# Block 0 of a fused attention and leaky-ReLU feed-forward kernel: one-level Strassen products in three of its four chunks, cut into slots, with the sums of w_out made there

## The chip, the cores and the metric

The kernel runs on one core of a Trainium2 chip. The metric is device time in microseconds for one execution, lower is better. The engines of the core are called here as the profile calls them: PE (TensorE, matmuls; PEld its weight loads), DVE (VectorE), ACT (ScalarE), POOL (GpSimd) and SP (SyncE, which here only issues transfers).

## The reference

A linear attention without softmax is followed by a feed-forward block with a leaky ReLU. The inputs q, k, v are float32; w_in and w_out are float64.

```python
# q, k, v: (8, 8, 576, 64) float32
kv  = einsum('bhsd,bhse->bhde', k, v)
out = einsum('bhsd,bhde->bhse', q, kv)
out = out / sqrt(mean(out * out, axis=-1) + 1e-6) * g_norm
x = out.transpose(0, 2, 1, 3).reshape(4608, 512)
h = x @ w_in                 # w_in (512, 2048) float64
g = maximum(0.01 * h, h)
y = g @ w_out                # w_out (2048, 512) float64, y (4608, 512)
```

## The kernel before

**Blocks and chunks.** The 4608 rows of x are worked in nine blocks of 512 rows (`NB = 9`). Within a block the 2048 hidden columns are four chunks (`NC = 4`); a chunk c has two halves h and two units u of 128 columns, so it needs four pieces of w_in (`w1_sb[h][c][:, u]`) and four of w_out (`w2_rows(h, c, u)`), 128x512 each.

**Weights.** The weights are read as 64-bit words and rounded to float32 on the chip. There are 32 jobs in the list `w_jobs`, one for each piece. For a job, `load_w` issues the transfer of 512 KB on SP into one of seven staging places, and `round_w` makes ACT convert the low word (L271, "add") and the high word (L269, "cut"), and then DVE clamp the high part (L273), shift it (L278), put its sign in (L280) and add the low part (L285). The first five jobs are rounded in `first_attention`; `first_block` calls `between` twice for every unit, and `between` loads and rounds the rest, two to three ahead of the unit that needs them. The jobs alternate between w_in and w_out.

**Block 0** (`first_block`) is the plain product. For each of 16 units n it computes one h tile of 128x512 (four matmuls of 512 columns), has ACT apply the leaky ReLU (L1353), and adds the product with w_out into four accumulators (`accs`), one unit late. Attention steps for block 1 and the tail of attention for block 0 are put in between by a dictionary of places.

**Block 1** uses one level of Strassen's method (Winograd's form, seven products): `product_h` computes a chunk of h, `product_o` a chunk of the output. Each of the seven products is 8 matmuls of 256 columns. A block is 28 slots, 7 for each chunk; in a slot one h product and, two slots behind (`LAG = 2`), one o product are issued. The sums that the products need are made by DVE and POOL: of x by `sides_x`, of w_in by `sides_w1` (four POOL additions of 128x512 a chunk), of w_out by `sides_w2` (four POOL additions a chunk, then written to DRAM for later blocks), of g by `sums_of` (four POOL additions a chunk). `combine` makes second-level sums of w_in for blocks 2 to 8, which use two levels for h.

**Order.** The instructions of each engine run in the order in which they are issued. `pin` keeps an instruction in the order of the program on its engine; all matmuls go through it (L121), and so do all steps of the rounding. `add` (L709) issues every sum, on DVE or POOL, and pins it if asked to or if `steady` is set. `put_off(n, f)` calls f after n slots.

Between block 0 and block 1 the kernel makes the sums of block 1's x on DVE, holds part of the w_in sums on POOL until the last weight is rounded (two copies of one element at L1405), and makes the w_out sums of chunk 0 on POOL; those of chunks 1 to 3 are made in block 1, each while `product_o` of the chunk before it runs.

Of the kernel before, what the change touches and what calls it, by code (L numbers as in the profile page):

```python
# [11 lines left out]
U32 = mybir.dt.uint32  # L12
I64 = mybir.dt.int64
# [11 lines left out]
def kernel(  # L25
# [41 lines left out]
    E = 32  # L67
# [26 lines left out]
    steady = first_done = in_line = False  # L94

    def in_turn(ins):

        if steady or in_line:
            pin(ins)

# [126 lines left out]
    def spare(n, name, dtype=F32):  # L227
# [3 lines left out]
    raw_homes = itertools.cycle([view(stage, i * NW, NW) for i in range(3)]  # L231
                                + [pair(i, NW) for i in range(4)])
# [15 lines left out]
    def load_f64(src, eng):  # L248
        raw = next(raw_homes).bitcast(U32)
        load(split(raw, src), src, eng)  # L250
        return raw.rearrange("p (n two) -> p n two", two=2)
# [44 lines left out]
    w_jobs[1:-1] = [w_jobs[i + 1 if i % 2 else i - 1] for i in range(1, len(w_jobs) - 1)]  # L296
# [3 lines left out]
    def load_w(j, *eng):  # L300
        eng = eng or (nc.sync,)
        dst, src = w_jobs[j]
        if w_in.dtype == I64:
            w_raws[j] = load_f64(src.bitcast(U32), eng)
        else:
            load(split(dst.rearrange("p a n -> p (a n)"), src) if len(src.shape) == 4 else dst,
                 src, eng)
# [5 lines left out]
    def round_w(j):  # L313
        for _ in rounding(j):
            pass

# [73 lines left out]
    def outputs(b, lo, hi, e, sums, kv=None):  # L390


        x, n = x_of(lo, hi), hi - lo
        tiles = att_tiles("o_ps")
        o_ps = [t[:, :n] for t in tiles]
        o_products(b, lo, hi, e, o_ps)
        if kv is not None:
            kv_beside(b + 1, kv, tiles)
        for l in range(2):
            sq = t2k(n, "sq" if e else f"sum{l}")  # L400
            nc.scalar.activation(sq, o_ps[l], func=AF.Square)
            if e == 0:
                sums.append(sq)
            else:
                in_turn(nc.vector.tensor_add(sums[l], sums[l], sq))
        for l in range(2):
            nc.scalar.activation(x[:, 2 * l + e, :], o_ps[l], func=AF.Copy, scale=g_sb[:, e:e + 1])

    def divide(lo, hi, sums):
# [3 lines left out]
        for l in range(2):  # L413
            t = t2k(n, "turned")
            in_turn(nc.vector.transpose(t, sums[l]))
            in_turn(nc.vector.tensor_reduce(rms[:, l, :], t.rearrange("p (a i) -> p a i", i=E),
                                            axis=AX.X, op=ALU.add))
            if l:
                act = nc.scalar.activation(rms, rms, func=AF.Sqrt, scale=1.0 / D, bias=eps_sb)
                if first_done:  # L420
                    pin(act)
            yield
        in_turn(nc.vector.reciprocal(rms, rms))
        spread = []
        for l in range(2):
            t = t2k(n, "spread")
            nc.scalar.copy(t.rearrange("p (a i) -> p a i", i=E),
                           rms[:, l, :].unsqueeze(2).to_broadcast([P, n // E, E]))
            spread.append(t)
# [11 lines left out]
    def both_outputs(b, lo, hi, sums, kv=None, banks=None):  # L441
# [9 lines left out]
        for l in range(2):  # L451
            sq = t2k(2 * n, "sq").rearrange("p (e n) -> p e n", e=2)
            nc.scalar.activation(sq, o_ps[l], func=AF.Square)
            sums.append(t2k(n, f"sum{l}"))
            squares.append(sq)
# [7 lines left out]
        for l in range(2):  # L463
            for e in range(2):
                nc.scalar.activation(x[:, 2 * l + e, :], o_ps[l][:, e, :], func=AF.Copy,
                                     scale=g_sb[:, e:e + 1])
# [50 lines left out]
    def attention(b, apart=True, fine=False):  # L517
# [17 lines left out]
        for m in range(2):  # L535
# [9 lines left out]
            if not apart and m == 0:  # L545
                for p in (2, 3):
                    load_pair(b, p)
# [154 lines left out]
    later, tick = [], 0  # L702
# [5 lines left out]
    def add(eng, out_, a, b_, minus=False, pinned=False):  # L708
        ins = eng.tensor_tensor(out_, a, b_, op=ALU.subtract if minus else ALU.add)  # L709
        if pinned or steady:  # L710
            pin(ins)

    def sides_w1(c):
# [4 lines left out]
        s12 = pair(0, U, 2, 2, P)  # L718
# [4 lines left out]
        def more():  # L723
            s34 = pair(1, U, 2, 2, P)
# [8 lines left out]
    writes = []  # L733

    def sides_w2(n):
# [7 lines left out]
        def sums(i):  # L743
            t = (t12, t34)[i]
            if n >= NC:
# [8 lines left out]
            if n == NC - 1:  # L754

                writes.append((w2_dram[c][i], t))
            else:
                pin(nc.sync.dma_start(w2_dram[c][i], t))
# [15 lines left out]
    def combine(c, part):  # L774
# [4 lines left out]
        parts = [((5, 6), pair(0, U, 2, 2, P))], [((7, 3), pair(1, U, 2, 2, P))], \  # L779
# [122 lines left out]
    def relu(t, src=None):  # L902
        with tc.issue_after(behind.pop()) if behind else nullcontext():
            nc.scalar.activation(t, t if src is None else src, func=AF.Prelu, alpha=SLOPE)  # L904
# [32 lines left out]
    def product_h(c, w_sides, x_sides, to):  # L937
# [3 lines left out]
        def done(i, bank):  # L941

            if i == 1:
                nc.scalar.copy(g11, bank)
            elif i == 5:
                nc.scalar.copy(g22, bank)
# [3 lines left out]
            elif i == 6:  # L950
                nc.scalar.copy(g21, bank)
# [16 lines left out]
    more = consts.tile([P, 19, P], F32, name="more")  # L968
# [185 lines left out]

    def product_o(n, g_sides, os, finish):
# [11 lines left out]
        def done(i, bank):  # L1167
# [9 lines left out]
            if i == 5:  # L1177
                sums(0)
            elif i == 4:
                sums(1)  # L1180
# [154 lines left out]
    def first_block(between):  # L1335

        accs = [ps_m.tile([P, DM], F32, tag=t, name="o_acc") for t in ("oa", "oc", "hb", "hd")]
        x, last = xTs.pop(0), None
        for n in range(2 * NC * U + 1):
            now = last  # L1340
            if n < 2 * NC * U:
                c, h, u = n // (2 * U), n // U % 2, n % U
                h_ps = ps_m.tile([P, NT], F32, tag=("ha", "hc")[n % 2], name="h_ps")

                parts = 2 if n == 0 else 1
                for part in range(parts):
                    cols = slice(part * NT // parts, (part + 1) * NT // parts)
                    for e in range(NE):
                        matmul(h_ps[:, cols], lhsT=w1_sb[h][c][:, u, e, :],
                               rhs=x[:, e, cols], start=(e == 0 and part == 0),  # L1350
                               stop=(e == NE - 1), skip_group_check=True)
                gT = view(g_all[n // 4 % 2], n % 4 * NT, NT)
                act = nc.scalar.activation(gT, h_ps, func=AF.Prelu, alpha=SLOPE)  # L1353
                if n == 2 * NC * U - 1:
                    pin(act)
                last = (gT, w2_rows(h, c, u), n)
            if now is None:
                continue
            between(n, 0)
            for t in range(4):  # L1360
                halves = now[2] // U % 2
                for v in range(1 + halves):
                    cols = slice(v * N2, v * N2 + N2) if halves else slice(0, NT)
                    matmul(accs[t][:, cols], lhsT=now[0][:, t * P:(t + 1) * P],
                           rhs=now[1][:, v, :],
                           start=(now[2] == 0), stop=(n == 2 * NC * U), skip_group_check=True)
            between(n, 1)
        for t in range(4):
            o = o_homes[t].rearrange("p u n -> p (u n)")
            if t % 2:  # L1370
                nc.scalar.copy(o, accs[t])
            else:
                nc.vector.tensor_copy(o, accs[t])
            nc.scalar.dma_start(out[t * P:(t + 1) * P, :], o)

    first_attention()
    steps = {i: tail for tail in [tail_of(0, NT, S)] for i in (6, 8, 10)}
    a_steps = attention(1, False)
    steps.update((i, a_steps)
                 for i in (12, 13, 15, 16, 19, 20, 22, 23, 24))  # L1380
    loaded, rounded = 7, 5

    def between(n, half):
        nonlocal loaded, rounded
        go(steps.get(2 * n + half, iter(())), 1)

        while half and rounded < min(3 * n + 8, 2 * n + 13, len(w_jobs) - (n < 11)):
            if loaded < len(w_jobs):
                load_w(loaded)
                loaded += 1  # L1390
                if loaded in (15, 19):
                    load_pair(1, (loaded - 15) // 4)
            round_w(rounded)
            rounded += 1
        if (n, half) == (12, 0):
            for p in range(2):
                load_pair(2, p)

    first_block(between)
    first_done = True  # L1400
    x_sides, _, sums, _ = sides_x(1)
    for _ in sums:
        pass
    for i, r in ((1, 0), (0, 1)):
        nc.gpsimd.tensor_copy(pair(i, U, 2, 2, P)[:1, 0, 0, r, :1], w2_1[:1, 1, NC - 1, U - 1, :1])  # L1405
    h_sides, more_h = sides_w1(0)
    more_h()
    for part in range(2):
        sides_w2(0)[1](part)
# [14 lines left out]
    LAG = 2  # L1424

    SPREAD = (2, 3, 9, 10, 12)
    o_queue, waited = collections.deque(), 0
# [8 lines left out]

    def go_o():
        while o_queue:
            if next(o_queue[0], o_queue) is not o_queue:
                return True  # L1440
            o_queue.popleft()

    for i in range(1, NB):
# [6 lines left out]
        for c in range(NC):  # L1450
# [7 lines left out]
            for t in range(7):  # L1458
                slot = 7 * c + t
                tick += 1  # L1460
                while later and later[0][0] <= tick:
                    later.pop(0)[1]()
# [39 lines left out]
                if slot == 4 and not one:  # L1502
                    while writes:
                        pin(nc.sync.dma_start(*writes.pop()))
# [85 lines left out]
```

## Time and profile before

| what | value |
|---|---|
| device time, median of 3 runs | 908.09 us (907.96 to 908.29) |
| device time of the profiled execution | 908.56 us |
| its span, first to last instruction | 906.6 us |
| PE busy in the span | 899.4 us (99%) |
| DVE, ACT, POOL busy in the span | 610.8 us (67%), 331.2 us (37%), 525.0 us (58%) |
| chain that ended last | PE 89%, DMA 4%, DVE 3%, POOL 2%, issue 1% |
| block 0's products | from 22.3 to 138.8 us of the span |
| granted TensorE clock | 1.00 throughout |

The device time is some 2 us above the span; the difference lies before the first and after the last instruction. A line of the timeline gives the start, the duration, the engine, the line of the kernel, the operation with what it writes and reads, how many instructions are merged in it, and in brackets the idle time before it with what ended it. The duration of an instruction includes time in which it waited for a port after it began, so intervals from start to start are used beside it.

### The profile page before, as it was taken

To read this page: it belongs to the slowest core of one execution; us is meant where nothing else is said; L and a number is where in the kernel's file an instruction comes from. 1 tells how busy PE (TensorE), PEld (TensorE's weight loads), DVE (VectorE), ACT (ScalarE), POOL (GpSimd) and SP (SyncE) were. 2 spreads that over 40 slices of the span, in tenths; PEclk is the share of its full clock that TensorE was granted. 3 is DMA by queue.
4 is the path that set the end of the run, shared out by engine and by line. 5 is a ranking of instruction groups with operands and counts; after the bars stand their busy time and mean duration, and the time that the engine had idled before them with its cause. 6 is when DMAs were issued, how large, how long until landed. Compare 5 with 4: busy or idle time off the path is not lost.

```text
span 906.6 us, 19091 instructions
## 1 busy us (share of the span) xinstructions
PE 899.4 (99%) x7344; PEld 789.7 (87%) x7344; DVE 610.8 (67%) x942; ACT 331.2 (37%) x645; POOL 525.0 (58%) x672
## 2 busy tenths in 40 slices
PE   8999999999999999999999999999999999999998
PEld 5555558888998999999999999999999999999997
DVE  5996856576674767685977498666877584646453
ACT  5663413231234332434333433343243424232420
POOL 2000255976738765766757584758477847883730
PEclk9999999999999999999999999999999999999999
DMA  9888436977799688968897798958886778677731
GB/s 322 260 260 266 151 98 195 306 251 244 253 306 329 204 279 256 307 219 261 252 322 263 218 298 255 321 170 271 250 284 188 230 207 277 203 234 226 258 111 59
DMA packets 109018, 219.00 MB, mean 242 GB/s; under 512 B 11264, under 2 KB 50560, under 8 KB 108928
## 3 DMA queue, kind: packets, MB, share of 16 engines
q1 hardware_dynamic: 105008, 212.22, 73.5%
q10 hardware_dynamic: 3472, 4.39, 1.4%
q8 instruction: 58, 0.95, 0.4%
q0 software_dynamic: 448, 1.18, 0.3%
q14 instruction: 32, 0.26, 0.1%
HBM read 187.34 MB, written 30.41 MB: 240 GB/s over the span
## 4 chain that ended last, share of the span: by engine, by line
PE 89%; DMA 4%; DVE 3%; POOL 2%; issue 1%; ACT 0%; SPq 0%; DVEq 0%; POOLq 0%; ACTq 0%
PE o_a L121 18%; PE o_c L121 14%; PE h_hd L121 9%; PE h_ha L121 9%; PE h_hc L121 9%; PE h_hb L121 8%; PE o_acc L121 6%; PE h_ps L121 6%; PE o_ps L121 3%; DMA q_in<-in_q_dram 2%; PE h_a L121 2%; PE h_b L121 2%; PE kv_ps L121 1%; PE h_d L121 1%; PE h_c L121 1%; DMA pairs<-in_v_dram 1%
## 5 line engine op out<-in xcount | busy, mean ns | idle before, releaser
L709 POOL TENSOR_TENSOR gs<-g 128x512 f32<-128x512 f32 x62 | 85.4, 1378 | 127.7 <-DVE w_all L709 60.3
L121 PE MATMUL o_a<-pairs,gs 128*128 128x256 f32 x472 | 111.9, 380 | 0.8 <-DMA pairs<-w 0.8
L709 DVE TENSOR_TENSOR o_all<-o_c,o_all 128x256 f32<-128x256 f32 (+2 forms) x124 | 69.4, 560 | 60.0 <-PE o_c L121 45.9
L904 ACT ACTIVATE g<-g 128x512 f32<-128x512 f32 x124 | 75.9, 631 | 62.4 <-DVE g L709 62.4
L709 DVE TENSOR_TENSOR g<-g,w_all 128x512 f32<-128x512 f32 (+1 forms) x84 | 87.9, 1046 | 15.2 <-POOL w_all L709 9.6
L709 POOL TENSOR_TENSOR w_all<-w_all 128x512 f32<-128x512 f32 x28 | 50.1, 1790 | 81.1 <-ACT w_all L1128 81.0
L121 PEld LDWEIGHTS o_a<-pairs,gs 128*128 128x128 f32 x472 | 85.5, 190 | 10.5 <-POOL more L709 1.0
L709 DVE TENSOR_TENSOR w_all<-h_ha,w_all 128x512 f32<-128x512 f32 x42 | 28.7, 684 | 55.0 <-PE h_ha L121 53.1
L1128 ACT COPY w_all<-h_hc 128x512 f32<-128x512 f32 x42 | 24.8, 590 | 105.9 <-PE h_hc L121 105.6
L1128 ACT COPY w_all<-h_ha 128x512 f32<-128x512 f32 x42 | 24.7, 587 | 104.5 <-PE h_ha L121 95.7
L121 PE MATMUL o_c<-pairs,gs 128*128 128x256 f32 x264 | 62.4, 379 | 0.0
L709 DVE TENSOR_TENSOR o_all<-o_a,o_all 128x512 f32<-128x512 f32 (+1 forms) x53 | 35.5, 669 | 37.5 <-PE o_a L121 36.8
L121 PE MATMUL o_a<-w,g 128*128 128x256 f32 x248 | 58.8, 379 | 0.0
L121 PE MATMUL h_ps<-xT,w_all 128*128 128x512 f32 (+1 forms) x136 | 58.1, 571 | 0.3 <-DVE w_all L285 0.3
L121 PE MATMUL o_acc<-w,g 128*128 128x256 f32 (+1 forms) x192 | 57.7, 451 | 0.0
L121 PEld LDWEIGHTS o_acc<-w,g 128*128 128x128 f32 x192 | 36.3, 190 | 21.5 <-issue 18.0
L709 DVE TENSOR_TENSOR g<-w_all 128x1024 f32<-128x1024 f32 x28 | 34.8, 1243 | 29.3 <-ACT w_all L1128 29.3
L709 POOL TENSOR_TENSOR pairs<-w 128x512 f32<-128x512 f32 x4 | 5.4, 1347 | 83.8 <-ACT cut L269 83.8
L121 PEld LDWEIGHTS o_c<-pairs,gs 128*128 128x128 f32 x264 | 47.9, 190 | 5.3
L121 PEld LDWEIGHTS o_a<-w,g 128*128 128x128 f32 x248 | 45.0, 190 | 4.9
L121 PEld LDWEIGHTS h_ps<-xT,w_all 128*128 128x128 f32 x136 | 25.4, 190 | 26.9 <-issue 24.9
L121 PE MATMUL h_hc<-stage,w_all 128*128 128x128 f32 x336 | 44.9, 276 | 0.0
(291 smaller groups left out, 2411.1 us busy)
## 6 DMA issues: line engine op xcount, KB each, us to landing
w_all<-w SPq DMA_DIRECT2D x196, 448.0 KB, 4.7
pairs<-w SPq DMA_DIRECT2D x94, 256.0 KB, 4.6
w<-w SPq DMA_DIRECT2D x22, 448.0 KB, 6.0
v_in<-in_v_dram SPq DMA_DIRECT2D x29, 288.0 KB, 5.6
k_in<-in_k_dram SPq DMA_DIRECT2D x28, 288.0 KB, 4.8
q_in<-in_q_dram SPq DMA_DIRECT2D x46, 144.0 KB, 4.8
q_in<-in_q_dram SPq DMA_DIRECT2D x46, 140.0 KB, 4.9
w<-stage SPq DMA_DIRECT2D x12, 512.0 KB, 3.6
```

The source lines that it names most:

```text
L121: pin(nc.tensor.matmul(*args, **kw))
L709: ins = eng.tensor_tensor(out_, a, b_, op=ALU.subtract if minus else ALU.add)
L904: nc.scalar.activation(t, t if src is None else src, func=AF.Prelu, alpha=SLOPE)
L1128: nc.scalar.copy(q[:, at], bank)
```

## The change

Block 0 keeps the plain product for chunk 0 alone. Chunks 1 to 3 go through `product_h` and `product_o`, in 21 slots laid out by hand; chunk 0's output product, in 16 pieces (one hidden unit of 128 by 128 rows each), is spread over the seven slots of chunk 1. The last nine output products of block 0 are issued beside the first nine h products of block 1, since the queue of output products now starts in block 0.

With it go these edits: `w_jobs` is put into the order in which chunks need the pieces; the staging places become seven for the first 7 jobs, five up to job 20 and three from there; from job 5 on `round_on` replaces `round_w`: it leaves a job half done until the next one starts, and for every even job and all from 20 on, ACT makes the shifted high part by a Prelu with integer output, so that DVE needs three instructions for it and not four; block 0's x sums (four) are made on POOL; the w_out sums of all four chunks are made on POOL in block 0 or just behind it and read back from DRAM in block 1; almost everything in block 0 is pinned (`in_first`, `lined`).

```diff
-    raw_homes = itertools.cycle([view(stage, i * NW, NW) for i in range(3)]
-                                + [pair(i, NW) for i in range(4)])
+    raw_homes = [view(stage, i * NW, NW) for i in range(3)] + [pair(i, NW) for i in range(4)]
+    FEW, LAST = 7, 20
+    def raw_home(j):
+        return raw_homes[j % 7 if j < FEW else (j - FEW) % 5 if j < LAST else (j - LAST) % 3]
-    w_jobs[1:-1] = [w_jobs[i + 1 if i % 2 else i - 1] for i in range(1, len(w_jobs) - 1)]
+    w_jobs = [w_jobs[8 * c + 2 * i + second] for second, c in
+              ((0, 0), (0, 1), (1, 0), (0, 2), (1, 1), (0, 3), (1, 2), (1, 3)) for i in range(2 * U)]
+    def end_w():
+        while half_way:
+            dst, add, cut, high, by_act = half_way.popleft()
...
+            if by_act:
+                pin(nc.scalar.activation(high.bitcast(I32), cut, func=AF.Prelu, scale=2.0 ** 60,
+                                         alpha=2.0 ** 127))
...
+            if by_act:
+                pin(nc.vector.scalar_tensor_tensor(high, in0=cut, scalar=3, in1=high,
+                                                   op0=ALU.logical_shift_left, op1=ALU.bitwise_or))
+            else:
+                pin(nc.vector.tensor_scalar(high, cut, 3, None, op0=ALU.logical_shift_left))
+                pin(nc.vector.scalar_tensor_tensor(high, in0=cut, scalar=0x80000000, in1=high,
+                                                   op0=ALU.bitwise_and, op1=ALU.bitwise_or))
...
+                pin(nc.vector.tensor_tensor(dst[:, i], high[:, i], add[:, i], op=ALU.add))
+    def by_act(j):
+        return j % 2 == 0 or j >= LAST
+    def round_on(j):
...
+        if j >= LAST:
+            end_w()
+        add, cut = own("add", U32), own("cut")
...
+        pin(nc.scalar.activation(add, raw[:, :, 0], func=AF.Copy, scale=2.0 ** -29))
+        pin(nc.scalar.activation(cut, raw[:, :, 1].bitcast(F32), func=AF.Copy, scale=2.0 ** -112))
+        pin(nc.vector.tensor_scalar(cut, cut, HIGH_MOST, -HIGH_MOST, op0=ALU.min, op1=ALU.max))
+        end_w()
+        half_way.append((dst, add, cut, high, by_act(j)))
     def sides_w2(n):
...
-            if n >= NC:
+            if n >= 0:
                 pin(nc.sync.dma_start(t, w2_dram[c][i]))
...
+            put_off(2, lambda: pin(nc.sync.dma_start(w2_dram[c][i], t)))
+    SUMS_OFF = {1 - NC: (4, 1), 2 - NC: (1, 1)}
...
+    ROUND_0 = 5, 6, 8, 9
+    ROUND = (11, 12, 14, 15, 17, 18, 20), (21, 22, 23, 24, 25, 26, 27), (28, 29, 30, 32)
+    TAIL_0 = 1, 2, 3
+    A_0 = 4, 5, 7, 8, 10, 11, 11, 12, 13, 14, 15
+    UNITS = 2, 2, 2, 3, 2, 3, 2
+    def first_block():
...
+        for n in range(2 * U):                      # chunk 0's h, plain
...
+            if n == 1:
+                for t, a, b_ in ((t1, b12, b11), (t2, b22, t1), (t4, b21, t2)):
+                    add(nc.gpsimd, t, a, b_, True)
+            round_to(ROUND_0[n])
+            gT = view(g_all[0], n * NT, NT)
+            pin(nc.scalar.activation(gT, h_ps, func=AF.Prelu, alpha=SLOPE))
...
+        w_sides, more_h = sides_w1(1)
+        add(nc.gpsimd, b12, b22, b12, True)
+        more_h()
...
+        pool = {2: lambda: sides_w2(-NC)[1](0), 3: lambda: sides_w2(-NC)[1](1),
+                8: lambda: w2_first(0), 9: lambda: w2_first(1)}
+        for c in range(1, NC):
+            n = c - NC
+            g_sides = {}
+            h_steps = product_h(n, w_sides, x_sides, g_sides)
+            for t in range(7):
+                slot = 7 * (c - 1) + t
+                later_steps()
+                if t < len(ROUND[c - 1]):
+                    round_to(ROUND[c - 1][t])
+                if slot in pool:
+                    pool[slot]()
+                go(h_steps, 1)
+                if c == 1:
+                    go(o_0, UNITS[t])
+                elif waited == LAG:
+                    go_o()
+                elif o_queue:
+                    waited += 1
+                if slot in TAIL_0:
+                    go(tail, 1)
+                go(a_steps, A_0.count(slot))
+                if t == 4:
+                    next_sides, more_h = sides_w1((c + 1) % NC)
+                elif t == 6:
+                    more_h()
...
+                if slot == 18:
+                    next_x, _, sums, _ = sides_x(1)
+                    go(sums, 2)
+                elif slot == 19:
+                    go(sums)
+            o_queue.append(product_o(n, g_sides, os, store(0)))
+            go(h_steps)
+            w_sides = next_sides
```

## The prediction

> **What bounds the kernel now.** I read the page first, then the waits of PE, then busy time by stretch, then the timelines of block 0. PE is the bound: it waits for hardly anything.
>
> ```profile
> PE   8999999999999999999999999999999999999998
> DVE  5996856576674767685977498666877584646453
> POOL 2000255976738765766757584758477847883730
> ```
>
> ```profile
> PE h_ps L121 <- DVE w_all L285: 0.3, 1, 0.3
> ```
>
> The second fence, from PE's waits, is its only wait inside block 0's products (0.3 us, for job 1). But in slices 2 and 3 DVE is full too, while POOL is idle. By stretch (columns: length, then busy us and instructions of PE, PEld, DVE, ACT, POOL, then clock and DMA):
>
> ```profile
> 24.00:64.00 40.00, 39.67 (x145) 21.15 (x144) 38.94 (x89) 25.65 (x51) 0.00 (x0) 1.00 0.94 283
> 64.00:112.00 48.00, 48.00 (x304) 26.24 (x303) 36.08 (x63) 20.48 (x36) 7.01 (x5) 1.00 0.64 197
> 140.00:235.00 95.00, 95.00 (x673) 81.44 (x672) 63.14 (x101) 29.16 (x61) 75.95 (x74) 1.00 0.77 244
> ```
>
> From 24 to 64 us DVE works 38.94 of 40 us with no POOL beside it. The change takes PE time out of this stage and puts DVE and POOL work in. What DVE's rounding costs (job 3), and PE's products:
>
> ```profile
> 28.45 0.42 DVE L273 TENSOR_SCALAR cut<-cut 128x512 f32<-128x512 f32 x1
> 28.90 0.43 DVE L278 TENSOR_SCALAR w_all<-cut 128x512 uint32<-128x512 uint32 x1
> 29.36 0.69 DVE L280 SCALAR_TENSOR_TENSOR w_all<-cut,w_all 128x512 uint32<-128x512 uint32 x1
> 30.09 0.69 DVE L285 CUSTOM_DVE_ANT_0 w_all<-w_all,add 128x1024 uint16<-128x1024 uint16 x1
> 29.88 3.60 PE L121 MATMUL o_acc<-w,g 128*128 128x512 f32 x8
> 33.31 3.60 PE L121 MATMUL h_ps<-xT,w_all 128*128 128x512 f32 x8
> 152.94 1.89 PE L121 MATMUL h_b<-xT,w_all 128*128 128x256 f32 x8
> 154.66 1.89 PE L121 MATMUL h_d<-xT,w_all 128*128 128x256 f32 x8
> ```
>
> From start to start a job takes 2.25 us of DVE; 8 matmuls of 512 columns take 3.43 us, of 256 columns 1.73 us. What happens when POOL adds beside DVE:
>
> ```profile
> 91.94 1.55 DVE L285 CUSTOM_DVE_ANT_0 w_all<-w_all,add 128x1024 uint16<-128x1024 uint16 x1
> 93.42 1.48 DVE L273 TENSOR_SCALAR cut<-cut 128x512 f32<-128x512 f32 x1
> 91.67 1.27 POOL L709 TENSOR_TENSOR pairs<-w,pairs 128x512 f32<-128x512 f32 x1
> 92.90 1.71 POOL L709 TENSOR_TENSOR pairs<-w,w 128x512 f32<-128x512 f32 x1
> 94.58 1.44 POOL L709 TENSOR_TENSOR pairs<-w,pairs 128x512 f32<-128x512 f32 x1
> ```
>
> The two take turns. The clamp that takes 0.42 us alone takes 1.48, ending (94.9) just behind the POOL addition that ended at 94.6; the next addition is then late (1.44 for 1.27). A DVE instruction with a PSUM operand isn't touched (0.69 us at 156.66, amid POOL work), nor a transpose (0.63 at 117.63). Per POOL addition DVE loses: 91.94 to 93.42 is 1.48 for 0.60 (0.88); 95.02 to 96.23 is 1.21 for 0.46 (0.75); 299.88 to 301.61 and on to 303.18 is 1.73 and 1.57 for 0.60 (1.13, 0.97). I take 1.0 us a turn, bounds 0.75 and 1.13.
>
> **PE's work.** Chunk by chunk: plain h is 4 x 3.43 = 13.74, Strassen 7 x 1.73 = 12.09, saved 1.65; plain o is 13.77 (its halves of 256 columns take 3.45), saved 1.68. Three chunks: 10.0 us. Products put beside block 1 are moved, not saved, and PE has no gap at the old boundary (h_a starts at 138.65 as o_acc ends), so nothing is won there.
>
> Without waits PE's times would be: chunk 0's h ends at 36.6 (as three runs of 3.43 behind 26.34); slots 0 to 6 add 12.09 + 13.77, 0.4 for the attention tail and 1.2 for kv, so slot 7 starts at 64.1; slots 7 to 20 add 24.18, twelve o products (20.7), 1.2 and 1.8 of attention: 47.9, end at 112.0.
>
> **DVE's work.** Intervals of dependent instructions: shift 0.46, sign 0.72, add 0.60; the clamp, now followed by another job's step, 0.34 (96.23 to 96.56). An odd job below 20 takes 2.12, one helped by ACT 1.66. From x's end at 24.0, up to the accumulator copy that slot 7's first product needs (its bank is the accumulator's): jobs 1 to 4 at 2.25, 9.0; six odd jobs (5 to 15) 12.7; six even ones 10.0; the clamp of 17, 0.3; three h sums 1.8; two transposes 2.2; one accumulator copy 0.6; the tail's sums and divide 1.8. Sum 38.4: DVE would reach that copy at 62.4, against 64.1. There is no slack even alone.
>
> For slots 7 to 20: jobs 17 and 19, 4.2; 18, 1.7; 20 to 31, 19.9; 6 h and 12 o sums at 0.60, 10.8; two transposes 2.2; kv copies 0.4; block 1's sums and divide as at 108.3 to 121.4 with the POOL turns taken out, 6.8; four x sums 2.4. Sum 48.4, against PE's 47.9.
>
> In two divides DVE also waits for ACT in line, as at 153.55 and 154.22 (0.37 and 0.47): 0.8 each.
>
> **POOL's turns.** Up to slot 7: three x sums (issued as soon as x is there, among jobs 1 and 2), five for chunk 1, four of w_out's chunk 0, two for chunk 2: 14. Slots 7 to 20: 2 + 4 + 4 + 4 + 4 + 4 + 4 = 26 (rest of chunk 2's w_in sums, two lots of g, w_out's chunks 1 and 2, w_in's chunk 3 and block 1's chunk 0). They delay DVE only where its instruction is one that takes turns: 32.7 of 38.4 us (85%) in the first part, 31.4 of 48.4 (65%) in the second. So 14 x 0.85 = 11.9 and 26 x 0.65 = 16.9 us.
>
> Then DVE ends part one at 24.0 + 38.4 + 0.8 + 11.9 = 75.1, part two at 75.1 + 48.4 + 0.8 + 16.9 = 141.2. PE, which needs DVE's sums bank by bank, ends slot 20 there and not at 112.0: **29 us of waits**. What is late next: ACT's ReLU behind each sum, and behind that, in line on ACT, the next job's conversions.
>
> The Trainium skill, SBUF — State Buffer, section "SBUF: two separate sides", says of the port pair that VectorE and GpSimd share that it is "an exclusive lock, not a bandwidth split", held for the whole instruction. With the 1.27 us of a lone addition in place of 1.0, the turns would be 36.6 us and not 28.8, the time 935, inside the forecast's own range; the trace shows less, since each turn begins before the other's recorded end.
>
> **What is small.** ACT's new Prelu with integer output isn't in the trace; ACT's float instructions of this size take 0.49 (PSUM) to 0.58 us from start to start, integer output included (L271, 0.57), so I take 0.57; 19 of them make 11 us of ACT, spread over 88 us, with bounds of plus or minus 1.7. In slots 0 to 6 ACT then has 11 jobs at 1.15, six Prelus at 0.57, seven h evictions (3.7), the tail (1.9) and a copy: 22 of 27.5 us, not the bound, but tight. A gain is excluded: it is an added instruction. w_out's twelve POOL sums leave block 1: nothing gained, PE doesn't wait there. In their place eight reads of 512 KB pass SP (3.6 to 6.3 us to land, two slots being 6.9 us): covered, and up to 4 us if they queue behind the w_in reads. SP's writes of w_out sums wait for POOL with weight loads behind them; five places of lead (some 10 us of rounding) cover a wait of 2 to 3 us. The new job order changes no byte.
>
> **Sum.** The profiled execution's 908.56 (span 906.6 plus 2 outside) - 10.0 + 29.2 = 927.8; the median stands 0.47 lower: **927.3 us**, slower by 2%.
>
> **Rivals.**
> 1. *The other side: DVE keeps up.* Turns then fall where DVE waits or is in PSUM work, and PE stays the bound: 898.1 with no wait, some 901 with three. It decides below 10 us of waits, that is if two thirds of the 28.8 us of turns vanish. For it: from 140 to 235 us POOL works 75.95 and DVE 63.14 of 95 us and PE never waits. Against: there no rounding stands in front of the sums, and DVE's own work here fills PE's time without any turn. 0.18.
> 2. *Turns cost half.* Shorter waits for sums that POOL issues while DVE idles: 908.1 - 10.0 + 14.8 = 913. 0.17.
> 3. *ACT and DVE in step.* The ReLU behind a late sum holds ACT, so the next conversion, so DVE: up to 1 us for each of nine h sums, 936. For: all of block 0 is pinned. Against: two jobs are in hand at a time. 0.15.
> 4. *A PE that has waited runs slowly.* The first filler matmuls run at half pace for 3.8 us under a granted clock of 1.00:
>
> ```profile
> 1.54 3.78 PE L121 MATMUL idle_ps<-g 128*128 128x512 f32 x4 [1.54 <-DVE group L323]
> 7.74 1.88 PE L121 MATMUL idle_ps<-g 128*128 128x512 f32 x4
> ```
>
> 0.95 us for one against 0.47: 1.9 us lost after a long wait, none after the 0.49 us at 12.5. Five waits of over 3 us would give 9.5: 937. 0.10. The Trainium skill, TensorE: Matmul & The Clock Gate, section "What's actually happening", puts the point at an idle window of about 3.4 us; no row here shows it.
> 5. *It is not what it says, or cancels:* 908. 0.02.
>
> Forecast 0.38, its own range 916 to 940. Slower: 0.38 + 0.17 + 0.15 + 0.10 = 0.80; faster 0.18; same, within 0.2% (about what a measurement of this kernel can tell from none), 0.02. The range 904 to 944 leaves out most of rival 1 and the sum of 3 and 4.
>
> **What would show it.** Right: PE waits for job 1 before the second h tile (3 us, POOL's x sums beside it), for job 8 at the first output piece, then for DVE's sums in slots 5 to 10; clamps of 1.4 us throughout block 0; block 1's first h near 141 us. Wrong: DVE with gaps before slot 10, POOL's sums in them, and block 1's first h at 112 to 122.

## The result, and the profile after

| | before | after |
|---|---|---|
| device time, median | 908.19 us | 948.76 us |
| ratio | | 1.046, 95% interval 1.042 to 1.050 |
| profiled execution: time, span | 908.56, 906.6 us | 948.43, 946.7 us |
| block 1's first h product starts at | 138.65 us | 160.66 us |

The change makes the kernel slower, by 40.6 us where 19 were forecast; the time lies above the forecast's range of 904 to 944 us. Medians here and below leave out one execution of 1164.8 us, in the sixth experiment, which ran in a slower state of the chip. The page again first: busy tenths in 40 slices of 23.7 us, then the chain of work that ended last.

```profile
PE   8796778999999999999999999999999999999998
...
DVE  5989888645647485768597759765977584655554
...
POOL 2335466664653676566666766576757766874730
PEclk9998897999999999999999999999999999999999
...
PE 82%; DVE 9%; DMA 3%; POOL 2%; ACT 2%; issue 2%; DVEq 0%; ACTq 0%; POOLq 0%; SPq 0%
```

The loss is in slices 2 to 7, where PE falls to 6 and 7 tenths, DVE is at 8 and 9, and the clock row falls with PE. DVE's share of the chain goes from 3% to 9%. PE's waits (us in total, times, longest), which were 0.3 us in block 0 before:

```profile
PE h_c L128 <- DVE g L771: 7.1, 1, 7.1
PE o_acc L128 <- DVE w L352: 4.4, 1, 4.4
PE h_b L128 <- ACT g L1011: 3.3, 1, 3.3
PE h_b L128 <- DVE g L771: 3.2, 1, 3.2
PE h_ps L128 <- DVE w_all L297: 3.0, 1, 3.0
PE h_d L128 <- ACT g L1006: 2.5, 1, 2.5
PE h_d L128 <- DVE g L771: 2.5, 1, 2.5
PE h_a L128 <- ACT g L1004: 2.2, 1, 2.2
PE h_a L128 <- DVE o_all L1482: 1.9, 1, 1.9
```

They have the forecast's names: job 1 (L297), job 8 at the first output piece (L352), then sums (L771). Each releaser is DVE, or an ACT step that came late behind DVE. By stretch (length; busy us and instructions of PE, PEld, DVE, ACT, POOL; granted clock, DMA share, GB/s):

```profile
24.00:64.00 40.00, 32.63 (x126) 18.71 (x125) 35.56 (x51) 21.61 (x42) 15.81 (x12) 0.91 0.67 196
64.00:112.00 48.00, 33.53 (x259) 27.29 (x258) 42.42 (x62) 21.84 (x42) 20.93 (x15) 0.86 0.70 205
24.49:160.66 136.17, 104.74 (x554) 75.55 (x553) 119.63 (x168) 65.53 (x124) 66.43 (x48) 0.87 0.59 176
```

From job 1's clamp to block 1's first h DVE is busy for 119.63 of 136.17 us; the missing 16.5 us turn out to be the part that the forecast lacked. Job 1 from the timeline of DVE, and POOL's x sums beside it:

```profile
24.49 1.21 DVE L285 TENSOR_SCALAR cut<-cut 128x512 f32<-128x512 f32 x1
25.73 1.38 DVE L290 TENSOR_SCALAR w_all<-cut 128x512 uint32<-128x512 uint32 x1
27.14 1.63 DVE L292 SCALAR_TENSOR_TENSOR w_all<-cut,w_all 128x512 uint32<-128x512 uint32 x1
28.81 0.69 DVE L297 CUSTOM_DVE_ANT_0 w_all<-w_all,add 128x1024 uint16<-128x1024 uint16 x1
29.42 0.42 DVE L285 TENSOR_SCALAR cut<-cut 128x512 f32<-128x512 f32 x1
```

```profile
24.12 1.28 POOL L771 TENSOR_TENSOR xt<-xT 128x512 f32<-128x512 f32 x1 [17.92 <-DVE xT L726]
25.48 2.74 POOL L771 TENSOR_TENSOR xt<-xT,xt 128x512 f32<-128x512 f32 x2
```

Three DVE steps beside three POOL additions take 1.24, 1.41 and 1.67 us from start to start; the clamp behind them, with POOL quiet, is back at 0.42. From PE's timeline, with the wait before each group in brackets:

```profile
29.55 12.26 PE L128 MATMUL h_ps<-xT,w_all 128*128 128x512 f32 x24 [3.00 <-DVE w_all L297]
...
82.27 1.99 PE L128 MATMUL h_a<-xT,w_all 128*128 128x256 f32 x8 [1.89 <-DVE o_all L1482]
...
100.74 3.78 PE L128 MATMUL h_c<-xt,more 128*128 128x256 f32 x8 [7.14 <-DVE g L771]
```

After the long waits eight matmuls take 3.78 us where 1.99 is normal: some 14 us in all of block 0 by such rows. What they cost in time is the subject of the fourth experiment.

DVE's own waits between 24.49 and 160.66 us, and ACT's largest between 22 and 161:

```profile
DVE cut L371 <- ACT cut L370: 4.2, 6, 1.7
DVE pairs L371 <- ACT pairs L370: 2.4, 3, 0.8
DVE pairs L344 <- ACT pairs L340: 2.2, 3, 0.8
DVE w_all L344 <- ACT w_all L340: 1.9, 2, 1.2
```

```profile
ACT g L964 <- DVE g L771: 30.7, 9, 5.6
```

DVE's clamp (L371) waits for ACT's conversion (L370), and its sign step (L344) for ACT's Prelu (L340), while ACT is held in front of its ReLUs (L964) by DVE's sums. In order of time, with other lines left out:

```profile
100.01 0.68 DVE L771 TENSOR_TENSOR g<-h_c,g 128x512 f32<-128x512 f32 x1
100.72 0.63 ACT L964 ACTIVATE g<-g 128x512 f32<-128x512 f32 x1 [3.61 <-DVE g L771]
...
101.26 0.61 ACT L340 ACTIVATE w_all<-pairs 128x512 int32<-128x512 f32 x1
...
101.90 0.69 DVE L344 SCALAR_TENSOR_TENSOR w_all<-pairs,w_all 128x512 uint32<-128x512 uint32 x1 [1.22 <-ACT w_all L340]
```

ACT stood for 3.61 us in front of the ReLU; the Prelu of the job in hand was queued behind it, and DVE then stood for 1.22 us for that Prelu.

### The profile page after: what moved, and what is told of

Same layout as the page of the kernel before. It is cut to its first block, busy times and chain, and to the rows that moved or that the text cites. A ratio compares the mean times of both kernels' runs of the same rounds, so it can differ in the third digit from the quotient of the medians.

```text
span 946.7 us, 19388 instructions
## 1 busy us (share of the span) xinstructions
PE 906.1 (96%) x7440; PEld 815.2 (86%) x7440; DVE 642.9 (68%) x953; ACT 346.3 (37%) x673; POOL 564.8 (60%) x698
## 4 chain that ended last, share of the span: by engine, by line
PE 82%; DVE 9%; DMA 3%; POOL 2%; ACT 2%; issue 2%; DVEq 0%; ACTq 0%; POOLq 0%; SPq 0%
PE o_a L128 20%; PE o_c L128 16%; PE h_hd L128 9%; PE h_ha L128 9%; PE h_hc L128 9%; PE h_hb L128 8%; PE o_ps L128 3%; DVE w L352 2%; PE h_a L128 2%; PE h_c L128 2%; PE h_ps L128 1%; PE h_b L128 1%; PE h_d L128 1%; DMA pairs<-in_v_dram 1%; POOL more L771 1%
## 5 line engine op out<-in xcount | busy, mean ns | idle before, releaser
L771 POOL TENSOR_TENSOR gs<-g 128x512 f32<-128x512 f32 x68 | 93.6, 1379 | 140.5 <-ACT g L964 62.5
L128 PE MATMUL o_a<-pairs,gs 128*128 128x256 f32 x504 | 121.4, 384 | 4.4 <-DMA pairs<-w 1.7
L771 DVE TENSOR_TENSOR o_all<-o_c,o_all 128x512 f32<-128x512 f32 (+2 forms) x135 | 76.9, 570 | 63.8 <-PE o_c L128 50.4
L964 ACT ACTIVATE g<-g 128x512 f32<-128x512 f32 x133 | 81.5, 631 | 103.3 <-DVE g L771 97.0
L128 PEld LDWEIGHTS o_a<-pairs,gs 128*128 128x128 f32 x504 | 92.4, 193 | 16.5 <-POOL stage L771 3.8
L771 POOL TENSOR_TENSOR w_all<-w_all 128x512 f32<-128x512 f32 x28 | 50.1, 1790 | 91.6 <-ACT w_all L1187 91.4
L771 DVE TENSOR_TENSOR g<-g,w_all 128x512 f32<-128x512 f32 (+1 forms) x84 | 88.7, 1056 | 14.2 <-POOL w_all L771 8.4
L128 PE MATMUL o_c<-pairs,gs 128*128 128x256 f32 x304 | 73.0, 384 | 0.0
L771 DVE TENSOR_TENSOR o_all<-o_a,o_all 128x512 f32<-128x512 f32 (+1 forms) x63 | 42.3, 671 | 42.5 <-PE o_a L128 41.8
L771 DVE TENSOR_TENSOR w_all<-h_ha,w_all 128x512 f32<-128x512 f32 x42 | 28.7, 684 | 54.9 <-PE h_ha L128 54.9
L128 PEld LDWEIGHTS o_c<-pairs,gs 128*128 128x128 f32 x304 | 56.4, 193 | 6.9
L771 DVE TENSOR_TENSOR g<-w_all 128x1024 f32<-128x1024 f32 x28 | 35.1, 1253 | 29.4 <-ACT w_all L1187 29.4
L771 POOL TENSOR_TENSOR gs<-gs,g 128x512 f32<-128x512 f32 x34 | 46.9, 1378 | 2.3
L771 POOL TENSOR_TENSOR gs<-g,gs 128x512 f32<-128x512 f32 x34 | 47.1, 1386 | 0.3
L128 PEld LDWEIGHTS h_ha<-stage,w_all 128*128 128x128 f32 x336 | 43.1, 192 | 1.8 <-issue 0.3
L128 PE MATMUL h_ha<-stage,w_all 128*128 128x128 f32 x336 | 44.4, 275 | 0.0
L128 PE MATMUL h_ha<-xT,w_all 128*128 128x128 f32 x224 | 43.9, 278 | 0.0
```

The lines of the kernel that those rows point to most:

```text
L128: pin(nc.tensor.matmul(*args, **kw))
L964: lined(nc.scalar.activation(t, t if src is None else src, func=AF.Prelu, alpha=SLOPE))
```

## The experiments

Where an expectation does not say otherwise, theory A is that DVE's queue (its own work, with POOL's turns in it) sets the end of block 0. Experiments 7, 10 and 11 edit the kernel before, the others the changed one (948.76 us), and medians are given. Ratios are to the kernel before on the same chip, with 95% intervals.

**1. Without POOL's sums in block 0.** Each product reads raw operands where a sum was wanted:

```diff
-        s12 = w1_sums(c, 0)
+        if in_first and c:
+            return {1: a11, 2: a12, 4: a22, 5: a21, 6: a22, 7: a11, 3: a12}, lambda: None
...   (the same for the sums of w_out, of x and of g)
```

> The changed kernel without POOL's sums in block 0: the operands of w_in's chunks 1 to 3, of w_out's four chunks, of block 0's x and g are used unsummed in their place (these sums are left out, and the same bytes of w_out go to DRAM). Everything else, the order on DVE and ACT included, stays. Theory A (DVE's queue: its own work fills PE's time, and POOL's turns of about 1 us each come on top): some 29 us of PE waits and most of the half-paced matmuls behind them go, 903 to 915 us, clamps back to 0.42 us. Rival B (DVE and ACT in step: a ReLU behind a late sum holds ACT, so the next conversion, so DVE): turns are not what matters, half of the 31 us of waits stay, 925 to 935 us.

Measured 931.51 us, ratio 1.026 (1.024 to 1.029): 17.2 us less, theory B's number, though the place of the ReLU is not the cause (experiment 3). DVE's stretch up to block 1's first h:

```profile
24.49:145.70 121.21, 99.74 (x553) 72.27 (x553) 98.14 (x167) 65.36 (x123) 22.58 (x19) 0.92 0.71 212
```

Its busy time falls by 21.5 us (119.63 to 98.14), its idle time rises from 16.5 to 23.1. So POOL's turns are real, but some of what they give back becomes waiting, and most of the loss does not need POOL.

**2. ACT's Prelu for every job**, which takes one DVE instruction out of each odd job below 20:

```diff
-        return j % 2 == 0 or j >= LAST
+        return True
```

> The changed kernel with ACT making the shifted high part for every job from 5 on (by_act always true): DVE has eight shifts less (8 x 0.46 = 3.7 us), ACT eight Prelus more (8 x 0.57 = 4.6 us). Theory A: DVE's queue is the bound, so 3 to 7 us faster (waits, and half pace behind them), 941 to 946 us. Rival B: ACT is the one that is late, so the same or slower, 948 to 953 us.

Measured 948.63 us, ratio 1.045 (1.043 to 1.046). That is in B's range, and yet in the profile block 1's first h starts 5.0 us earlier (155.66). DVE's waits for ACT in the rounding hardly grow (11.4 us against 10.9). Two waits of PE in block 1 (1.3 and 0.6 us) that the changed kernel does not have take part of the gain back, and the median does not follow: inconclusive by itself.

**3. Block 0's ReLUs one slot later**, so that a late sum holds up no conversion behind its ReLU:

```diff
                 add(nc.vector, g11, bank, g11, pinned=True)
-                relu(g11)
+                relu_of(g11)      # held until the next slot; also for g21 and g22
```

> The changed kernel with the three ReLUs that follow a DVE sum in each chunk of block 0 issued one slot later, behind the next slot's conversions, so that ACT is not held by a late DVE sum. Theory A: DVE is the bound whatever ACT does, 944 to 951 us. Rival B: up to 1 us for each of nine sums and the half pace behind it, 930 to 940 us.

Measured 947.61 us, ratio 1.044 (1.041 to 1.046): A. The edit does what it is meant to: ACT's waits in front of its ReLUs fall from 30.7 to 7.3 us. But DVE's waits for ACT in the rounding only fall from 10.9 to 9.4 us, so where the ReLU stands in ACT's order is not the cause. PE's waits only move (h_c's for its sum is 8.7 us).

**4. Filler matmuls in PE's waits**, 25 calls, so that PE is not idle ahead of the real ones:

```diff
+    FILL = {9: (2, "hb"), 10: (8, "hb"), 18: (3, "ha"), 19: (3, "ha")}
+    FILL_O = {0: (5, "hd"), 18: (1, "ha")}
+                if slot in FILL:
+                    fill(*FILL[slot])
```

> The changed kernel with 25 filler matmul calls of 512 columns (0.86 us each at full pace, results unused) placed on PE where it waited: three before the second h tile, five before chunk 0's first output piece, two in slot 9, eight in slot 10, four in slot 18, three in slot 19. Theory C (after a wait of 3 us and more PE runs at half pace for some 3.5 us, in all about 14 us): 8 to 13 us faster, 936 to 941 us, no 8-matmul group of 3.4 us or more except at slot 4 where no bank is free. If the half pace comes from anything but the waits: no gain, 948 to 956 us.

Measured 949.39 us, ratio 1.045 (1.043 to 1.046): no gain. From 24 to 64 us PE is now busy for 39.36 us at a granted clock of 1.00 (32.63 at 0.91 after), and a wait of 5.4 us for a DVE sum follows. From 64 to 112 us the clock is still 0.89, and some 6 of the 14 us of slow matmuls remain. Block 1's first h starts at 157.62, 3.0 us earlier; then PE waits in block 1, for a sum of DVE's (1.3 us) and for w_out's sums read back from DRAM (2.6 us), and the time is the same. So most of the slow matmuls run in time in which DVE's queue would have kept PE waiting; what the other 6 us cost was not tested.

**5. DVE's rounding cut down.** From job 5 on, clamp, shift and sign are left out; the last add, all of ACT's steps and all of POOL's sums stay:

```diff
-            if by_act:
-                pin(nc.vector.scalar_tensor_tensor(high, in0=cut, scalar=3, in1=high, ...
-            else: ...
+            if not by_act:
+                high = cut
-        pin(nc.vector.tensor_scalar(cut, cut, HIGH_MOST, -HIGH_MOST, op0=ALU.min, op1=ALU.max))
```

> The changed kernel with block 0's weight rounding on VectorE cut down from job 5 on: the clamp and the shift and sign steps are left out and only the last add of each job stays (so the weights are not the reference's). ScalarE's copies, its Prelu and all of POOL's sums stay. By the rows of the changed kernel this takes some 18 us of clamps and 32 us of shifts and signs out of VectorE's 112 us in block 0. Theory A (VectorE's queue sets block 0; everything else only shows inside its waits): 900 to 910 us, block 1's first h at 112 to 122, the slow matmul stretches gone but for the first one near 29.5. Theory B (ScalarE in step with VectorE, or POOL's sums, hold matmuls also when VectorE has half its work): 915 to 930 us, with waits for ScalarE's g at the o products as the largest rows.

Measured 919.42 us, ratio 1.012 (1.010 to 1.014): 29.3 us less, in B's range. Block 1's first h starts at 129.25:

```profile
24.49:129.25 104.76, 94.71 (x552) 69.67 (x551) 73.79 (x104) 64.72 (x123) 60.20 (x47) 0.95 0.73 228
```

DVE's work falls by 45.8 us and the stretch by 31.4. DVE is the main cause, but with 31 us of idle time on DVE block 0 is still 16 us longer than without any wait (138.65 - 10.0 - 15.5 for the nine moved products = 113.1): PE waits for jobs 1 and 8 (3.0 and 2.0), for ACT's g in the last slots (2.8 and 1.9), and runs slowly behind these waits. A as put (900 to 910) left that out. The edit takes the clamp's hand-over from ACT to DVE away too, so the 29.3 us are not the price of DVE's work alone.

**6. The last rounds later.** The last four jobs in slots 15 to 19:

```diff
-    ROUND = ..., (28, 29, 30, 32)
+    ROUND = ..., (28, 29, 29, 30, 31, 32)
```

> The changed kernel with the last rounds of chunk 3 spread over slots 15 to 19 instead of 14 to 17, so that the matmuls' sums of chunk 3's h tiles stand ahead of more of the rounding in VectorE's and ScalarE's queues. The work is the same. Theory A1 (the last rounds stand ahead of the sums that the last slots' matmuls wait for, and some 9 us of matmuls follow the last round): 939 to 946 us, block 1's first h 3 to 9 us earlier. Theory A2 (the sum of VectorE's work sets the end wherever the rounds stand): 947 to 951 us, waits in slots 14 to 20 moved but not less.

Measured 948.45 us, ratio 1.044 (1.042 to 1.046): A2. The profile shows why: block 1's first h starts 10.1 us earlier (150.57), further than A1 forecast, but the next product then waits and runs slowly.

```profile
150.57 1.89 PE L128 MATMUL h_a<-xT,w_all 128*128 128x256 f32 x8
155.91 3.78 PE L128 MATMUL o_c<-w,gs 128*128 128x256 f32 x8 [3.45 <-DVE o_all L771]
```

A second wait for a DVE sum, of 3.38 us at 178.63 with slow matmuls behind it, takes the rest back: the same queue gives the same end, wherever the rounds stand.

**7. POOL's turns by themselves.** The kernel before, with 40 additions in block 0 that nobody reads:

```diff
+            if 2 <= n < 12:
+                for _ in range(4):
+                    pin(nc.gpsimd.tensor_tensor(more[:, :4, :], more[:, 4:8, :], ..., op=ALU.add))
```

> The kernel before with 40 additions of 128x512 on POOL, which nobody reads, put into block 0's loop beside the weights' rounding (four in each of ten steps), and a memset ahead of them. It measures by itself what POOL's additions take from VectorE. If each takes 0.75 to 1.0 us from VectorE, its busy time up to 112 grows by 30 to 40 us, where it has some 13 us of idle time: 918 to 938 us. If they cost about half of that or less: 908 to 918 us.

Measured 931.50 us, ratio 1.025 (1.024 to 1.027): 22.9 us more. Whole-run busy time from the page, first of before, then of this kernel:

```profile
PE 899.4 (99%) x7344; PEld 789.7 (87%) x7344; DVE 610.8 (67%) x942; ACT 331.2 (37%) x645; POOL 525.0 (58%) x672
```

```profile
PE 906.7 (98%) x7344; PEld 791.4 (85%) x7344; DVE 651.0 (70%) x942; ACT 331.6 (36%) x645; POOL 584.7 (63%) x713
```

The same 942 DVE instructions take 40.2 us more: 1.0 us per POOL addition, the price that the prediction took for a turn. DVE's spare time took 17 of the 40 us. The page SBUF — State Buffer of the Trainium skill, section "SBUF: two separate sides", which lets the lock be held for a whole instruction, would make it up to the length of the addition; these additions are recorded with 1.49 us each and cost 1.0.

**8. Rounding that waits for nothing of ACT's.** DVE does the same instructions in the same order, but reads a weight tile that is already there; ACT does all its steps:

```diff
-        pin(nc.vector.tensor_scalar(cut, cut, HIGH_MOST, ...
+        pin(nc.vector.tensor_scalar(cut, w1_sb[0][0][:, 0].rearrange("p e n -> p (e n)"), HIGH_MOST, ...
...   (likewise the sign step and the last add read this tile; ACT writes its results beside it)
```

> The changed kernel, where VectorE's rounding in block 0 has the same instructions, sizes and order but reads nothing that ScalarE made (it reads a weight tile that is already there; the weights are so not the reference's), and ScalarE does its copies and its Prelu all the same. VectorE no longer waits for ScalarE in the rounding, so some 9 to 12 of its 14 us of waits go. Theory A (the step between the two engines costs what VectorE waits): 935 to 941 us. Theory B (these waits lie where VectorE's queue would wait for matmuls anyway): 945 to 950 us.

Measured 940.10 us, ratio 1.035 (1.033 to 1.036): 8.7 us less, A. The stretch to block 1's first h:

```profile
24.49:150.58 126.09, 99.72 (x555) 72.28 (x553) 119.39 (x167) 67.39 (x124) 66.80 (x48) 0.92 0.62 189
```

DVE's busy time is the same (119.39 against 119.63) and the stretch is 10.1 us shorter. That is what the hand-over between the two engines costs. It is not all DVE's side of it: ACT's waits for DVE's last adds (8.4 us in the changed kernel) go as well, since DVE no longer reads ACT's buffers.

**9. Both cuts of 1 and 5 at once.**

> The changed kernel with both cuts at once: block 0's POOL sums left out (raw operands in their place) and VectorE's rounding from job 5 on cut down to the last add (so the output is not the reference's). If the saving in matmuls is 10.0 us as summed and VectorE's queue is the only loss: 898 to 903 us. If a loss stays that belongs to the slots' order itself (a wait for ScalarE's g ahead of each h or o tile): 905 to 912 us.

Measured 912.43 us, ratio 1.004 (1.003 to 1.006), just above the second case. Even with POOL's sums and nearly half of DVE's work gone (65.8 us busy), the change does not pay for itself. PE's largest waits are now:

```profile
PE o_a L128 <- DMA pairs<-w: 3.3, 1, 3.3
PE h_d L128 <- ACT g L1004: 2.9, 1, 2.9
PE kv_ps L128 <- DMA v_in<-in_v_dram: 2.2, 1, 2.2
```

The first (at 180 us, in block 1) is for w_out's sums read back from DRAM, the third for a transfer of v. The second still comes out of the rounding: ACT's copy of an h tile stands behind the conversions and Prelus of the last jobs, which waited for DVE's last adds (1.9 and 1.2 us).

**10 and 11. Strassen where the rounding is nearly over**: the kernel before, with chunk 3 alone changed (a saving of at most 3.3 us), and then a mended form.

```diff
-        for n in range(2 * NC * U + 1):
+        LASTN = 2 * (NC - 1) * U
+        for n in range(LASTN + 1):
...
+    h_steps = product_h(-1, w_sides, {1: b11, 2: b21, 3: b22, 4: t4, 5: t1, 6: t2, 7: b12}, g_sides)
+    go(h_steps)
+    o_queue.append(product_o(-1, g_sides, os, store(0)))
```

> The kernel before with one-level Strassen in chunk 3 of block 0 alone, where the weights' rounding has ended; chunks 0 to 2 stay plain. It takes one of the change's three savings (3.3 us of matmuls at most) without its cost in VectorE's queue. Theory A (VectorE's queue was the whole cost): 904.5 to 907 us. If POOL's sums for chunk 3 and the later start of block 1's own sums bring a wait of their own: 907 to 914 us.

Measured 919.59 us, ratio 1.012 (1.010 to 1.014), above both ranges. The first form waits in two places, of which the second is the changed kernel's wait for job 1 again, with the same x sums on POOL beside it:

```profile
PE h_b L121 <- DVE o_all L1374: 8.1, 1, 8.1
PE h_ps L121 <- DVE w_all L285: 3.0, 1, 3.0
```

> Strassen in chunk 3 of block 0 alone, mended where the run before it waited (8.1 us for VectorE's copies of the plain accumulators behind an attention divide, 3.0 us for job 1 beside POOL's x sums): ScalarE copies the two accumulators whose banks Strassen's first h tiles take, the last three steps of block 1's attention move behind the first h tiles, and POOL's x sums wait for the tenth h. Theory A (those two waits were the whole loss): 919.6 - 8.1 - 3.0 - 3.7 of half pace = 904.8, so 904 to 907 us. Rival (VectorE's and ScalarE's work near the end of the rounding is itself too much once chunk 3's matmuls are shorter, so that the wait moves to another tile): 908 to 915 us.

Measured 915.13 us, ratio 1.008 (1.007 to 1.009): the upper end of the rival's range. Both waits are gone (0.3 us is left for job 1), and others of 8.5 us together stand in their place:

```profile
PE o_c L121 <- DVE o_all L710: 3.6, 1, 3.6
PE h_a L121 <- DVE xT L436: 1.7, 1, 1.7
...
PE h_b L121 <- DVE g L710: 1.3, 1, 1.3
PE h_d L121 <- DVE g L710: 1.2, 1, 1.2
```

Each is again DVE's. No version was found that beats the kernel before.

## Where the prediction held, and the step that failed

**Right: the sign, the engine and the first places.** DVE as the new bound and the waits for jobs 1 and 8 and then for sums are as argued (PE's saving of 10.0 us is a count that no run shows by itself); rival 1 (DVE keeps up) and rival 2 (turns at half, 913) are out. PE waits for job 1 by the 3.0 us that the text named. That this wait is the x sums' is borne out by the first experiment (0.3 us without them) and the tenth and eleventh (3.0 us again with them beside job 1, 0.3 us with them later). Two signs missed: PE also waits in slots 17 to 19 (2.5, 3.3, 1.3 and 2.5 us), and the clamps take 1.2 us and more in only 6 of 31 jobs, not throughout.

**Right in size: DVE's work.** "DVE's work" and "POOL's turns" came to 38.4 + 48.4 + 28.8 = 115.6 us; DVE was busy for 119.6. The turn of 1.0 us is what experiment 7 measured. The first experiment agrees with the forecast's share of turns: it takes 29 POOL instructions and 21.5 us of DVE's time out of the stretch, 0.74 us each, where the forecast had 28.8 us for 40. Three of block 1's x sums took 1.5 to 1.7 us from start to start beside POOL, where the sum had 0.60.

**The step that failed: "In two divides DVE also waits for ACT in line: 0.8 each".** These 1.6 us were all the waiting that the sum gave DVE. It was idle for 16.5 us. Against the forecast's own sum, for the profiled execution:

| term | forecast | measured | difference |
|---|---|---|---|
| DVE's start | 24.0 | 24.5 | +0.5 |
| its work, turns included | 115.6 | 119.6 | +4.0 |
| its idle time | 1.6 | 16.5 | +14.9 |
| block 1's first h | 141.2 | 160.66 | +19.4 |
| from there to the end of the time | 786.6 | 787.8 | +1.2 |
| time | 927.8 | 948.4 | +20.6 |

10.9 of the 16.5 us stand in DVE's list of waits as the rounding's for ACT, and experiment 8 took 8.7 us off the time by taking these waits away. So the two engines do run in step, and the cost comes on top of DVE's work. Rival 3 had that mechanism and set it against the forecast instead of adding it to it, and it put the cause at the ReLUs; moving them (experiment 3) changed nothing. The step lies in the rounding itself, which crosses from ACT to DVE at the clamp and, for every job helped by Prelu, a second time. "Two jobs are in hand at a time", the reason given against it, did not keep DVE busy: up to job 19 one job stands half done while the next is converted, and DVE waits all the same; from job 20 on only one is in hand, and Prelu, sign step, last add, next conversion and clamp follow one behind the other, as DVE's rows show:

```profile
148.08 0.69 DVE L344 SCALAR_TENSOR_TENSOR pairs<-pairs 128x512 uint32<-128x512 uint32 x1 [0.70 <-ACT pairs L340]
148.80 0.76 DVE L352 CUSTOM_DVE_ANT_0 w<-pairs 128x512 uint16<-128x512 uint16 x2
150.35 0.43 DVE L371 TENSOR_SCALAR pairs<-pairs 128x512 f32<-128x512 f32 x1 [0.79 <-ACT pairs L370]
151.47 0.69 DVE L344 SCALAR_TENSOR_TENSOR pairs<-pairs 128x512 uint32<-128x512 uint32 x1 [0.69 <-ACT pairs L340]
```

From one sign step to the next are 3.39 us, and in 1.48 of them DVE waits for ACT. The other idle time (waits for a divide's steps, for PE and for the squares, and gaps too short for the list) was not separated by a run.

**Rival 4, the slow matmuls, is there and costs little here.** Some 14 us of half-paced matmuls were recorded, more than the 9.5 us priced. With some 8 us of them gone block 0 ended 3.0 us earlier and the time was the same (experiment 4). A slow PE is no term to be added in full when another engine sets the pace.

**A small term put at nothing.** The forecast called the reads of w_out's sums covered, or worth up to 4 us if they queue. In the changed kernel PE waits 1.7 us for one of them in block 1 (at 214.82), and 2.5 to 3.3 us in experiments 4, 5, 8 and 9. This lies in the +1.2 us behind block 0.

## What to carry to other kernels

When a change makes another engine the bound, sum that engine's idle time as carefully as its work: every crossing to a third engine in a pipeline that is only one step deep is a wait that nothing covers any more. A cut in matmuls was worth nothing here, where the vector engine was already at 97% in the first part of the stage. Moving work within such a stage mostly moves the wait: the reorderings of experiments 3 and 6 changed nothing, and the one of experiment 11 won 4.5 us and left 8.5 us of waits.

## What the runs showed of the hardware

- A POOL addition of 128x512 that runs beside DVE's rounding took 1.0 us from DVE (40.2 us for 40 additions), less than its own recorded 1.49 us. In the changed kernel it was 0.74 us (21.5 us for 29 POOL instructions).
- The half pace after a wait does not follow from that wait's length alone. A wait of 3.00 us (29.55) and one of 2.24 us (88.22) were followed by it in the changed kernel, one of 3.29 us in the second experiment and one of 3.05 us in the eighth were not. TensorE: Matmul & The Clock Gate of the Trainium skill, section "What's actually happening", puts it down to an idle window of about 3.4 us that runs freely in time. A free-running window agrees with the waits over 3 us that go unpunished; a whole idle window does not fit into the single wait of 2.24 us, and no run here tells what decided there.
